# Moving the key one-hot turn, and the query turns behind it, one attention step on

## The chip, the cores and the metric

The kernel runs on one core of a Trainium2 chip. The time is that of the device for one execution, in microseconds (us); the median over several executions is quoted. "PE" is the matmul engine, "DVE" the vector engine, "ACT" the scalar engine, "POOL" gpsimd and "SP" the sync engine, which here only issues transfers.

## The reference

Clustered attention (4 batches, 8 heads, 768 positions, head size 64, 16 clusters), then a mixture of 4 experts. The part that matters is how a query sees only the keys of its own cluster:

```python
q_assign = np.argmax(np.einsum('bhsd,hcd->bhsc', q_n, c_n), axis=-1)
k_assign = np.argmax(np.einsum('bhsd,hcd->bhsc', k_n, c_n), axis=-1)
mask = q_assign[:, :, :, None] == k_assign[:, :, None, :]
scores = np.where(mask, scale * np.matmul(q, k.transpose(0, 1, 3, 2)), -1e9)
...
attn = np.exp(scores - max); attn = attn / (sum + 1e-9)      # then attn @ v
...
h = np.maximum(x @ w1[e], 0.0)                               # e = 0..3
out += p[:, e:e + 1] * (h @ w2[e])
```

## The kernel before

Every instruction stream is ordered by hand. The mask is folded into the score matmul: below the 64 rows of a key (tile `kf`) and a query (tile `qf`) lie 16 more rows with the one-hot of its cluster. To make them, the kernel scores positions against centroids, takes the maximum, compares (tile `oh`), transposes the one-hot on PE (the "turn") and copies the result from PSUM into rows 64 to 79. For the first batch this is side work, tied to attention steps.

```python
def onehot(self, shifts=1):                 # the key turn: 6 transposes for shifts=2
    self.ot = self.bank(BF16)
    for x in range(shifts):
        for c0 in range(0, self.w, 128):
            nc.tensor.matmul(self.ot[...], self.oh[:, c0 + x*CL : c0 + x*CL + 128], identb,
                             is_transpose=True)
def put(self, j, r, on): ...                # copy 16 rows of head j, half r, into kf (DVE or ACT)
def keep(self, on="dve"):                   # copy the whole turned tile into SBUF tile oht
    self.oht = asg.tile([128, QW], BF16, name="oht", bufs=2)
    self.move(self.oht[:, :self.w], self.ot[:, :self.w], on)
def send(self, j, r):                       # a transfer from oht into the rows of kf
    (... nc.sync).dma_start(out=self.rows(slice(D, D + CL), j, r), in_=self.oht[...])
# ... onehot_narrow, put_narrow: the same for one query block, 8 transposes and DVE copies
```

`k1` is the keys of heads 4 to 7 (local heads 0 to 3), `qb` the first query block of these heads, `qc` more queries of heads 0 to 3. So heads 4 and 5 get their rows by DVE copies (`puts`, two each), heads 6 and 7 by four transfers from `oht`.

One attention step is two (later four) score matmuls into one of two score banks `ps_s`, an exp on ACT into tile `at`, and the four value matmuls of the step two earlier (`LAG = 2`):

```python
for x, (h, y) in enumerate(...): nc.tensor.matmul(sp[...], KF..., QF...)   # score bank, 2 buffers
nc.scalar.activation(at, sp, ACT.Exp, scale=scale)
queue.append(pv); flush(LAG); tick()
# ...
at_step = {
    # ...
    5: lambda: (k1.back(), k1.top(), qb.back(), qb.top(), ...),
    7: lambda: (k1.onehot(2), puts(k1, 0), k1.keep(), k1.send_all((2, 3))),
    8: lambda: (qb.onehot_narrow(), qb.put_narrow(slice(0, 2), "dve")),
    9: lambda: (puts(k1, 1), qb.put_narrow(slice(2, HG), "dve")),
    11: lambda: qc.turn(0, dve, True),
    12: lambda: (qc.turn(1, dve, True), load_w(1)),
    14: lambda: (casts(qc, (0, 1)), qc.scores(dve)),
    # ...
}
while step < 3 * PER_U // 4 + LAG + D_T:
    at_step.pop(step, lambda: None)()       # side work of this step first,
    one_step()                              # then the next attention step
```

The softmax here doesn't subtract the row's maximum and nothing guards it: scores larger than these inputs give would overflow.

Of the kernel before, what the change touches and what calls it, by code (L numbers as in the profile page):

```python
# [20 lines left out]
def kernel(  # L21
# [27 lines left out]
    HG = H // 2  # L49
# [24 lines left out]
    act, dve, pool = nc.scalar.copy, nc.vector.tensor_copy, nc.gpsimd.tensor_copy  # L74
# [732 lines left out]
    k0, k1 = Assign(0, 1, 0, ("s", "mo", "mo", "mo")), Assign(0, 1, 1, ("s", "misc"))  # L807
    qa, qb = Assign(0, 0, 0, ("av",), 0, 1), Assign(0, 0, 1, ("mo",), 0, 1)
# [26 lines left out]
    def puts(x, j):  # L835
        for r in range(2):
            x.put(j, r, "dve")
# [27 lines left out]
    def late_casts():  # L865
        for j in range(HG):
            cast_v(0, 1, (j,))
            if j < 2:
                casts(k1, (2 + j,))
# [4 lines left out]
        3: lambda: (k1.scores(act), qb.scores(dve), puts(k0, 3)),  # L874
        5: lambda: (k1.back(), k1.top(), qb.back(), qb.top(),
                    qb.cast(0, 0, pool), qb.cast(0, 1, pool), late_casts()),
        7: lambda: (k1.onehot(2), puts(k1, 0), k1.keep(), k1.send_all((2, 3))),
        8: lambda: (qb.onehot_narrow(), qb.put_narrow(slice(0, 2), "dve")),
        9: lambda: (puts(k1, 1), qb.put_narrow(slice(2, HG), "dve")),
        11: lambda: qc.turn(0, dve, True),  # L880
        12: lambda: (qc.turn(1, dve, True), load_w(1)),
        14: lambda: (casts(qc, (0, 1)), qc.scores(dve)),
# [81 lines left out]
```

## Time and profile before

| | before |
|---|---|
| median of the first three runs | 472.22 us (472.22 to 472.25) |
| span of the profiled run | 470.4 us |
| PE busy | 463.2 us, 98% |
| holes of PE between 17 and 25 us | 0.41 (DVE's one-hot), 0.28 (ACT), 0.27 (a send) |

Besides the lines in the prediction, three of PE in the kernel before serve as marks below. In lines of the trace the columns are start in us, length in us, engine, line, operation, tiles, shape and count, and in brackets the idle time before the line and what ended it.

```profile
14.95 0.43 PE L267 MATMUL ps_mo<-t32q,bdc 128*32 128x128 f32 x8
...
22.91 0.78 PE L267 MATMUL ps_mo<-t32q,bdc 128*32 128x256 f32 x8
...
26.72 0.23 PE L692 MATMUL ps_mo<-identb,xn 128*128 128x128 bf16 x1 [0.28 <-DVE xn L685]
```

The first is the narrow query score matmul, the last shared landmark before the moved work (from here on "the mark"); the last is an output transpose (it turns a finished attention tile `xn`) after all of it. I call the time from the one to the other **the stretch**: 26.72 - 14.95 = 11.77 us here. It leaves out most of how a run started. The middle line is the next query score matmul, which reads two query copies of DVE (`t32q`).

### The profile page before, as it was taken

Reading aid. Unit: us, or ns where it says so; the run is one execution under the profiler, and the core shown is the slowest. Engines: PE = TensorE matmul, PEld = TensorE weight load, DVE = VectorE, ACT = ScalarE, POOL = GpSimd, SP = SyncE. Lnnn points to the kernel's source line nnn. Section 1 sums busy time; section 2 is a strip of 40 time slices with the busy share of each in tenths; the row PEclk is TensorE's granted clock in tenths of the full one; section 3 lists DMA queues with packets and bytes.
Section 4 is the critical chain, followed back from the end, with each engine's and each line's share of the span. In section 5 each row is a group of like instructions: output and inputs, shape, how many; then the busy total and the mean of one; then the engine's idle time right before and its main releaser. Section 6 shows DMA issues by size and latency. Waiting matters only on the chain.

```text
span 470.4 us, 11349 instructions
## 1 busy us (share of the span) xinstructions
PE 463.2 (98%) x4505; PEld 329.1 (70%) x4505; DVE 227.4 (48%) x554; ACT 276.9 (59%) x502; POOL 194.8 (41%) x301
## 2 busy tenths in 40 slices
PE   8999999999999999999999999999999999999996
PEld 5778777767767766777776667766766666667665
DVE  5964723542325563321234463523778767674112
ACT  5767675445655655566565656656665675664342
POOL 5936779275355593450433942000233232230000
PEclk9999999999999999999999999999999999999999
DMA  8999966996645941503666844220100100100101
GB/s 277 262 211 339 216 99 120 236 127 182 144 68 127 182 114 32 144 18 61 169 123 127 133 106 151 71 75 11 52 13 8 54 11 10 33 29 11 46 2 45
DMA packets 82381, 49.85 MB, mean 106 GB/s; under 512 B 57944, under 2 KB 77080, under 8 KB 82328
## 3 DMA queue, kind: packets, MB, share of 16 engines
q1 hardware_dynamic: 73080, 39.80, 35.1%
q0 software_dynamic: 8576, 9.25, 11.0%
q8 instruction: 35, 0.57, 0.5%
q14 instruction: 18, 0.15, 0.1%
q10 hardware_dynamic: 672, 0.08, 0.1%
HBM read 37.31 MB, written 6.30 MB: 93 GB/s over the span
## 4 chain that ended last, share of the span: by engine, by line
PE 95%; DVE 2%; DMA 1%; issue 0%; ACT 0%; SPq 0%; ACTq 0%
PE ps_mo L739 36%; PE ps_mo L758 35%; PE ps_s L649 9%; PE ps_av L676 7%; PE ps_s L562 1%; DMA kf<-oht 1%; PE ps_misc L562 1%; PE ps_s L87 1%; PE ps_mo L406 1%; PE ps_mo L242 1%; PE ps_misc L406 1%; DVE kf L315 1%; PE ps_misc L242 1%; PE ps_mo L267 0%; PE ps_misc L267 0%; DVE oh L287 0%
## 5 line engine op out<-in xcount | busy, mean ns | idle before, releaser
L655 ACT ACTIVATE at<-ps_s 128x512 bf16<-128x512 f32 x252 | 147.6, 596 | 115.5 <-PE ps_s L649 100.1
L739 PE MATMUL ps_mo<-xT,w1b 128*128 128x256 bf16 (+1 forms) x1664 | 195.9, 264 | 0.0
L758 PE MATMUL ps_mo<-w2b,hT 128*128 128x512 bf16 (+2 forms) x784 | 190.0, 375 | 0.0
L739 PEld LDWEIGHTS <-w1b 128*128 128x128 bf16 x1664 | 146.1, 98 | 24.8 <-issue 1.2
L745 ACT ACTIVATE hT<-ps_mo 128x512 bf16<-128x512 f32 x192 | 114.7, 598 | 60.5 <-PE ps_mo L739 57.7
L767 DVE SCALAR_TENSOR_TENSOR oacc<-ps_mo,psb,oacc 128x512 f32<-128x512 f32 (+1 forms) x74 | 54.3, 734 | 125.3 <-PE ps_mo L758 125.1
L758 PEld LDWEIGHTS <-hT 128*128 128x128 bf16 x784 | 66.9, 98 | 57.8 <-issue 3.1
L649 PE MATMUL ps_s<-qf,kf 80*128 80x256 bf16 (+1 forms) x456 | 82.7, 267 | 0.8 <-ACT at L655 0.4
L676 PEld LDWEIGHTS <-at 128*128 128x128 bf16 x1152 | 69.9, 97 | 15.3 <-issue 1.7
L676 PE MATMUL ps_av<-vx,at 128*128 128x65 bf16 x1152 | 80.3, 193 | 0.0
L662 POOL TENSOR_TENSOR at<-at,same 128x512 bf16<-128x512 bf16 x24 | 28.2, 1177 | 98.5 <-ACT at L655 83.0
L649 PEld LDWEIGHTS <-kf 80*128 80x128 bf16 x456 | 42.1, 98 | 20.6 <-issue 1.4
L380 POOL COPY t<-t 128x768 uint16<-128x768 uint16 x40 | 44.3, 1127 | 0.0
L579 DVE TENSOR_SCALAR same<-qf,late 128x256 bf16<-128x256 bf16 x144 | 39.0, 323 | 0.0
L662 DVE TENSOR_TENSOR at<-at,same 128x512 bf16<-128x512 bf16 x48 | 21.6, 450 | 25.9 <-ACT at L655 25.9
L364 POOL COPY h<-raw 128x768 uint16<-128x768 uint16 x24 | 20.3, 864 | 30.4 <-DMA raw<-in_k_dram 16.7
L361 POOL COPY h<-raw 128x768 uint16<-128x768 uint16 x16 | 13.1, 829 | 39.3 <-DMA raw<-in_q_dram 32.3
L765 DVE TENSOR_SCALAR oacc<-ps_mo,psb 128x512 f32<-128x512 f32 x18 | 13.5, 748 | 27.0 <-PE ps_mo L758 27.0
L683 DVE RECIPROCAL zr<-ps_av 128x4 f32<-128x4 f32 (+1 forms) x50 | 8.9, 178 | 33.3 <-PE ps_av L676 33.2
L336 POOL DMA_DIRECT2D qf<-oht x40 | 20.4, 519 | 7.5 <-DVE oht L313 3.9
L422 POOL COPY st<-sct 128x384 uint16<-128x384 uint16 x16 | 11.0, 736 | 28.8 <-DMA sct<-scs 28.8
L685 DVE TENSOR_TENSOR xn<-ps_av,zr 128x256 bf16<-128x256 f32 (+1 forms) x50 | 20.7, 414 | 1.7
(130 smaller groups left out, 263.2 us busy)
## 6 DMA issues: line engine op xcount, KB each, us to landing
raw<-in_v_dram SPq DMA_DIRECT2D x8, 768.0 KB, 5.4
out_dram<-oacc SPq DMA_DIRECT2D x23, 256.0 KB, 2.0
raw<-in_k_dram SPq DMA_DIRECT2D x7, 768.0 KB, 7.5
raw<-in_q_dram SPq DMA_DIRECT2D x6, 768.0 KB, 5.7
w1b<-in_moe_w_dram POOLq DMA_DIRECT2D x4, 1024.0 KB, 12.3
w2b<-in_moe_w_dram POOLq DMA_DIRECT2D x4, 1024.0 KB, 17.6
qf<-nos SPq DMA_DIRECT2D x2, 768.0 KB, 5.2
xT<-xn SPq DMA_TRANSPOSE x80, 2.4
```

The source lines that it names most:

```text
L336: (nc.gpsimd if self.b or self.i0 and self.g else nc.sync).dma_start(out=self.rows(slice(D, D + CL), j, r), in_=self.oht[p0:p0 + CL, :self.w])
L380: pool(self.all[:, y * w:(y + 1) * w].bitcast(U16)[:, z::2], self.t16[:, (2 * z + y) * w:(2 * z + y + 1) * w])
L579: nc.vector.tensor_scalar(same[:, x * 256:(x + 1) * 256], clusters(b)[:, g, w, k // 2, k % 2, :], key_nos[b % 2][:, g, 8 * i + 4 * (k // 2 ...
L649: nc.tensor.matmul(sp[:, x * n:(x + 1) * n], KF[b % 2][:K, h, r, i * 128:(i + 1) * 128], QF[b % 2][:K, h, rs[0]:rs[-1] + 1, w * 128:(w + 1 ...
L655: nc.scalar.activation(at, sp, ACT.Exp, scale=scale)
L662: (nc.gpsimd if n4 in POOL_STEPS else nc.vector).tensor_tensor(at, at, same_cluster(b, w, cur), op=ALU.mult)
L676: nc.tensor.matmul(av[:, h % 2, m, :], at[:, c0:c0 + 128], VX[b % 2][:, h, 2 * i + r, :], start=(first and x == 0 and m == 0), stop=(last ...
L685: nc.vector.tensor_tensor(xn[:, :nr].rearrange("p i j d -> p j i d"), av[:, :, :, :D], zr.broadcast_to([128, 2, nr, D]), op=ALU.mult)
L739: nc.tensor.matmul(ph[:, x * n:(x + 1) * n], W1[e][:, i, (f + x) * 128:(f + x + 1) * 128], xT[:, i, :], start=(i == 0), stop=(i == ND - 1))
L745: nc.scalar.activation(ht, ph, ACT.Relu)
L758: nc.tensor.matmul(po, hT[f // per][:, c0:c0 + 128], W2[e][:, f, c], start=(f == 0), stop=(f == NF - 1))
L767: nc.vector.scalar_tensor_tensor(oacc[:, c], po, pap, oacc[:, c], op0=ALU.mult, op1=ALU.add)
```

## The change

The intent is to fill the hole that PE has before the key turn: one step more of attention is issued ahead of it.

```diff
-        7: lambda: (k1.onehot(2), puts(k1, 0), k1.keep(), k1.send_all((2, 3))),
-        8: lambda: (qb.onehot_narrow(), qb.put_narrow(slice(0, 2), "dve")),
-        9: lambda: (puts(k1, 1), qb.put_narrow(slice(2, HG), "dve")),
+        8: lambda: (k1.onehot(2), puts(k1, 0), k1.keep(), k1.send_all((2, 3))),
+        9: lambda: (qb.onehot_narrow(), qb.put_narrow(slice(0, 2), "dve")),
+        10: lambda: (puts(k1, 1), qb.put_narrow(slice(2, HG), "dve")),
```

## The prediction

> **What bounds the kernel now.** I began with the page, to see which engine fills the span, and then cut the span into stretches to find where that engine is not full. The columns after the stretch are its length, then busy microseconds with the number of instructions for PE, PEld, DVE, ACT and POOL, then the granted clock, the DMA share and GB/s.
>
> ```profile
> PE 463.2 (98%) x4505; PEld 329.1 (70%) x4505; DVE 227.4 (48%) x554; ACT 276.9 (59%) x502; POOL 194.8 (41%) x301
> ...
> 16.00:20.00 4.00, 3.56 (x53) 3.04 (x51) 3.79 (x13) 2.90 (x6) 3.67 (x8) 1.00 1.11 233
> 20.00:24.00 4.00, 3.74 (x55) 3.09 (x55) 3.75 (x12) 2.97 (x6) 3.84 (x7) 1.00 1.20 213
> 24.00:24.75 0.75, 0.48 (x10) 0.29 (x7) 0.59 (x3) 0.60 (x1) 0.69 (x2) 1.00 1.26 214
> 24.75:28.00 3.25, 2.75 (x44) 2.23 (x45) 1.92 (x8) 2.52 (x5) 0.97 (x2) 1.00 1.20 214
> 28.00:60.00 32.00, 31.83 (x426) 25.83 (x426) 19.17 (x51) 21.21 (x40) 19.17 (x34) 1.00 1.11 254
> 60.00:120.00 60.00, 60.00 (x603) 43.73 (x602) 22.26 (x38) 34.04 (x60) 41.97 (x66) 1.00 0.79 149
> ```
>
> From 28 us on PE is filled almost without a hole, at full clock, so whatever PE gains or loses before that goes one for one into the end. The moved steps lie between 17 and 21 us. There PE has holes, while DVE (3.79 and 3.75 of 4.00) has nearly none and the DMA engines are full (share above 1). The third view is PE in order of time: start, length, instruction, and in brackets the idle time before it and what ended it.
>
> ```profile
> 16.88 0.38 PE L649 MATMUL ps_s<-qf,kf 80*128 80x256 bf16 x2
> 17.09 0.28 PE L676 MATMUL ps_av<-vx,at 128*128 128x65 bf16 x4
> 17.79 0.51 PE L296 MATMUL ps_misc<-identb,oh 128*128 128x128 bf16 x6 [0.41 <-DVE oh L287]
> 18.14 0.38 PE L649 MATMUL ps_s<-qf,kf 80*128 80x256 bf16 x2
> ...
> 20.26 0.38 PE L649 MATMUL ps_s<-qf,kf 80*128 80x256 bf16 x2 [0.28 <-ACT at L655]
> ...
> 24.75 0.22 PE L649 MATMUL ps_s<-qf,kf 80*128 80x128 bf16 x1 [0.27 <-DMA kf<-oht]
> ```
>
> The line at 17.79 is the moved turn: six transposes of the key one-hot (oh). PE stood 0.41 us before it because DVE had not finished oh. That hole is what the change aims at. Two more matter: 0.28 us for an exp of ACT at 20.26, and 0.27 us at 24.75 for rows of kf that come by DMA. The fourth view, the chain of waits through this stretch, tells which holes count.
>
> ```profile
> 17.18 0.57 DVE oh L287
> 17.75 0.05 issue
> 17.79 0.52 PE ps_misc L296 x6
> 18.31 0.02 issue
> 18.34 0.61 DVE kf L315 x2
> 18.95 0.01 issue
> 18.96 0.37 DVE oht L315
> 19.33 0.01 issue
> 19.35 0.62 SPq L336
> 19.97 0.04 issue
> 20.01 4.60 DMA kf<-oht
> 24.62 0.14 issue
> 24.75 0.22 PE ps_s L649
> ```
>
> The chain does not run along PE's attention work. It runs from oh through the moved turn, two copies into kf, the copy kept for the sends (oht), the sync engine's issue, and a transfer that takes 4.60 us to land, into the score matmul at 24.75.
>
> **What the Trainium skill says.** "Perfetto Trace Analysis", section "DMA Instruction — HWDGE (DVE, Sync)", says that the profiled length of such an issue leaves out the movement of data. The trace agrees: 0.62 us of issue, 4.60 us to landing. "DMA: Bandwidth & Descriptors", section "Issuing engines are not separate DMA queues", says that transfers from the scalar, sync and gpsimd engines interleave on the same 16 engines. That fits the full share while expert weights are loading by the software queue; it is my reading of why 12 KB needs 4.60 us. "TensorE: Matmul & The Clock Gate", its table of specifications, says that only weight loads are pulled ahead in TensorE's queue. The hole at 17.79, with the ready work of step 8 right behind it, is what this would give.
>
> **The change, part by part.** Three entries of the table that ties side work to attention steps move on by one: the key turn with its copies and four sends from 7 to 8, the first half of the narrow query turn from 8 to 9, the rest from 9 to 10. Nothing is added or removed. The compiled order says the same: PE has the same 8578 rows, ACT, POOL and SP are unchanged, and on DVE only one pair moves. An entry at n is issued just before step n+1, so one step (2 score matmuls, 4 value matmuls) moves ahead of the key turn, another ahead of the narrow turn, another ahead of the last entry. From the turn of the next queries at 20.60 on, PE's order is as before.
>
> *The hole at 17.79.* The step that moves forward takes PE about 0.35 us (0.40 from the scores at 16.48 to the next at 16.88, 0.35 from those at 15.31 to those at 15.66). But it can't start where the hole begins. There are two score banks, so step 8 writes the bank of step 6, whose exp must have ended. ACT in a short stretch shows:
>
> ```profile
> 16.23 1.26 ACT L655 ACTIVATE at<-ps_s 128x512 bf16<-128x512 f32 x2
> 16.90 1.08 ACT L655 ACTIVATE at<-ps_s 128x512 bf16<-128x512 f32 x2
> ```
>
> The second of the first pair is the first of the second pair: step 6's exp, from 16.90 to 16.23 + 1.26 = 17.49. With 0.05 us for the release (step 7's scores start at 16.88, an exp after 16.23 + 0.60 = 16.83), step 8's scores start at 17.54. The scores' issue takes 17.09 - 16.88 = 0.21 us, and the four value matmuls 0.12 us (from 15.54 and 19.35 to what follows them; once, at 18.36, it is 0.21). So the key turn can start at 17.54 + 0.33 = 17.87. oh lets it start at 17.79. The hole is filled, and the turn is 0.08 us later.
>
> *The hole at 20.26.* ACT now has step 8's scores about 0.4 us sooner, so I expect this 0.28 us to vanish too. PE then reaches 20.60's work about 0.35 + 0.28 = 0.6 us early.
>
> *DVE.* Before the key copies it is free at 18.25 (17.96 + 0.29) and starts them at 18.34. It would start at 18.42, and oht, the issues and the transfers all slip by 0.08 us. A reciprocal and a product (0.18 + 0.42 us) then pass ahead of the copies for head 5, which end near 21.1 and not 20.41; head 5 is read at about 22.5, so nothing waits. DVE has the same sum to do and reaches the query copies of 21.42 and 22.32 as late as before.
>
> *The transfer.* Four sends go out at 0.6 us pitch and land 0.6 us apart: by the same 4.6 us the second, third and fourth would land near 24.6, 25.2 and 25.9, which is where the score matmuls of heads 6 and 7 stop in the trace. All work up to 24.75 is the same in both kernels. So the 0.6 us that PE has won is spent waiting there: the hole of 0.27 becomes about 0.8 us, and the matmul starts near 24.83.
>
> *Sum.* -0.35 -0.28 (holes closed), +0.63 (waiting for the same transfer), +0.08 (the transfer later): +0.08 us, 472.22 to 472.3.
>
> **Rivals.** (a) The transfers don't bind: the PE gain stays, and the time falls by up to 0.41 + 0.28 = 0.69 us to 471.5. For it: these are real PE holes and PE bounds the rest. Against it: PE already waits for kf at 24.75, so arriving sooner cannot help. (b) The turn goes a whole step later, with oht and the sends: +0.35 to +0.5 us, to 472.7. For it: the change reads so. Against it: the step fits into the hole but for 0.08 us. It would take an exp that is late. (c) The transfers meet the weight load differently. They queue behind bulk loads, so 0.1 us in the issue may become some tenths in the landing, either way: 472.0 to 472.7. (d) A bank or DVE becomes the wait: the narrow turn and the last copies come later, and the second query turn needs the bank that head 5's copies read until about 21.1. PE could then stand there, but all before 24.75 is covered by the transfer.
>
> **Range and chances.** The runs before lie within 0.03 us, so the range is about mechanism: 471.9 (part of rival a, or a luckier landing) to 472.7 (b or c). I predict 472.3 us. Two per cent is 9.4 us; all holes of this stretch together are far below it. Faster by over 2%: 0.01; within 2%: 0.98; slower: 0.01.
>
> **What would show it.** Right: the key turn without a hole over 0.1 us before it and starting at 17.8 to 17.9; no ACT wait near 20; DVE's oht ending near 19.4; a wait of 0.6 to 1.0 us for kf before a score matmul at 24.7 to 24.9; after it the same picture as before, shifted by under 0.2 us. Wrong: no larger wait for kf, or kf landing by more than 0.3 us elsewhere, or a new hole after 28 us, which I expect nowhere.

## The result, and the profile after

The changed kernel took 472.66 us (median of 4 runs: 472.24, 472.51, 472.82, 472.92), the kernel before 472.24 us (4 runs, 472.22 to 472.28). The ratio is 1.0008, with a 95% interval of 0.9991 to 1.0025: the same at 2%, and not told apart from no change at all. (A ratio is the mean time of one kernel's fast runs over that of the other's of the same rounds, so not quite the ratio of the medians.) All outputs are right. The profiled run was the slowest of the four, 472.92 us, with a span of 471.1 us. PE in it:

```profile
15.25 0.43 PE L267 MATMUL ps_mo<-t32q,bdc 128*32 128x128 f32 x8
...
17.84 0.38 PE L649 MATMUL ps_s<-qf,kf 80*128 80x256 bf16 x2 [0.17 <-ACT at L655]
...
18.18 0.50 PE L296 MATMUL ps_misc<-identb,oh 128*128 128x128 bf16 x6
...
21.52 0.66 PE L242 MATMUL ps_misc<-ident,raw 128*128 128x128 f32 x4 [0.24 <-DVE kf L315]
...
22.80 1.38 PE L267 MATMUL ps_mo<-t32q,bdc 128*32 128x256 f32 x8
...
25.12 0.22 PE L649 MATMUL ps_s<-qf,kf 80*128 80x128 bf16 x1 [0.21 <-DMA kf<-oht]
...
26.75 0.33 PE L649 MATMUL ps_s<-qf,kf 80*128 80x128 bf16 x3 [0.45 <-DMA kf<-oht]
...
27.09 0.23 PE L692 MATMUL ps_mo<-identb,xn 128*128 128x128 bf16 x1
```

The key turn has no hole before it any more; the score matmul ahead of it waited 0.17 us for an exp of ACT. The ACT wait of 0.28 us that came near 20 us is gone. So PE did win time. It lost it again in three places that were not there before or were smaller: 0.24 us before the second query turn, whose bank head 5's copies still read; about 0.6 us inside the query score matmuls (1.38 us and not 0.78); and two waits for sends.

The longer query score matmuls are explained by DVE. Its two query copies, first in the kernel before, then in the changed one:

```profile
21.42 0.68 DVE L252 COPY t32q<-ps_mo 128x512 f32<-128x512 f32 x1
22.32 0.69 DVE L252 COPY t32q<-ps_misc 128x512 f32<-128x512 f32 x1
```

```profile
21.95 0.69 DVE L252 COPY t32q<-ps_mo 128x512 f32<-128x512 f32 x1
22.81 0.68 DVE L252 COPY t32q<-ps_misc 128x512 f32<-128x512 f32 x1
```

Counted from each run's own mark, they start at 6.47 and 7.37 us before, at 6.70 and 7.56 us after: DVE is 0.2 us later, while PE came 0.4 us earlier (22.91 - 14.95 = 7.96 against 22.80 - 15.25 = 7.55). PE started these matmuls early and stood in the middle of them until the second copy was done at 23.49.

Of the 0.70 us between the two profiled spans (471.1 - 470.4), 0.30 lie before the change has begun (15.25 - 14.95). The stretch is 27.09 - 15.25 = 11.84 us, 0.07 longer. Then 0.20 come between that output transpose and the next (26.72 to 28.35 before, 27.09 to 28.92 after), behind the last send, which landed late. The remaining 0.13 us are spread over the rest and I have no cause for them.

The 0.30 us are in the very first matmuls, which are the same in both kernels. Nine fp32 transposes of keys, before and after:

```profile
4.63 1.74 PE L242 MATMUL ps_mo<-ident,raw 128*128 128x128 f32 x9
```

```profile
4.58 2.08 PE L242 MATMUL ps_mo<-ident,raw 128*128 128x128 f32 x9
```

In both, single matmuls of this shape take about 0.42 us at first and 0.27 us from some moment on; the moment is later in the second trace. The Trainium skill, "TensorE: Matmul & The Clock Gate", section "What's actually happening", says that the clock is released by a free-running activity window, so that the release varies from run to run. The durations fit this, but the granted-clock column reads 1.00 here, so I call it the likely cause and not a shown one.

### The profile page after: what moved, and what is told of

It reads as the page before. It is cut to its first block, busy times and chain, and to the rows that moved or that the text cites. A ratio compares the mean times of both kernels' runs of the same rounds, so it can differ in the third digit from the quotient of the medians.

```text
span 471.1 us, 11349 instructions
## 1 busy us (share of the span) xinstructions
PE 463.6 (98%) x4505; PEld 329.6 (70%) x4505; DVE 227.7 (48%) x554; ACT 277.0 (59%) x502; POOL 194.7 (41%) x301
## 4 chain that ended last, share of the span: by engine, by line
PE 96%; DVE 1%; DMA 1%; SPq 0%; issue 0%; ACT 0%
PE ps_mo L739 36%; PE ps_mo L758 35%; PE ps_s L649 10%; PE ps_av L676 8%; PE ps_s L562 1%; DMA kf<-oht 1%; PE ps_mo L242 1%; PE ps_misc L562 1%; PE ps_s L87 1%; PE ps_mo L406 1%; PE ps_misc L267 1%; PE ps_misc L242 1%; PE ps_mo L267 1%; PE ps_misc L406 1%; PE ps_mo L276 0%; SPq L336 0%
```

## The experiments

The differences are 0.1 us in 472, and a run's start moves by more, so the stretch is the main reading and the median the second. What the start or the stretch gains does come through one for one, as the prediction assumed: in 12 of the 14 traces the span ends 443.7 us (within 0.1) after the stretch does. The two others are the first trace of the changed kernel (444.0, the late last send) and the run with later sends (445.0, see there). Some of the short stretches below belong to late marks, so pairs with like marks weigh most. "Largest landing" is the longest time from issue to landing among the four sends of `kf`. All were timed in 5 rounds (6 runs for one of them); the kernel before ran 38 times in all, 472.04 to 473.04, median 472.22.

| run | mark at | key turn after mark | stretch | largest landing | median |
|---|---|---|---|---|---|
| before | 14.95 | 2.84 | 11.77 | 4.7 | 472.24 |
| before again (e10) | 14.86 | 2.84 | 11.89 | 4.7 | 472.22 |
| changed | 15.25 | 2.93 | 11.84 | 5.0 | 472.66 |
| changed again (e1) | 15.22 | 2.93 | 11.93 | 5.1 | 472.45 |
| changed again (e9) | 14.72 | 2.93 | 11.96 | 4.9 | 472.30 |
| key turn alone (e2) | 14.83 | 2.93 | 11.92 | 4.8 | 472.27 |
| queries alone (e3) | 14.96 | 2.84 | 11.69 | 4.6 | 472.25 |
| changed, sends first (e4) | 15.24 | 2.93 | 11.47 | 4.7 | 472.21 |
| before, sends first (e5) | 14.83 | 2.83 | 11.79 | 5.7 | 472.09 |
| before, sends first (e11) | 15.40 | 2.84 | 11.29 | 4.7 | 472.21 |
| key turn alone, sends first (e6) | 15.06 | 2.93 | 11.36 | 4.7 | 471.94 |
| key turn alone, sends first (e12) | 15.11 | 2.93 | 11.36 | 4.8 | 471.96 |
| before, sends later (e7) | 14.89 | 2.84 | 12.49 | 5.0 | 473.28 |
| changed, sends first, head 5 on ACT (e8) | 15.32 | 2.93 | 11.25 | 4.7 | 472.03 |

The theory under test: the sends (one-hot, key turn, copies, `oht`, four issues, landing) end last in this stretch, and the change delays them by the 0.08 us by which the key turn slips. The main rival: DVE's order and the bank (reciprocal and product ahead of head 5's copies, later query copies) set the end.

### The changed kernel again, and the kernel before again

No edit.

> The changed kernel unaltered, for the scatter of its time and a second trace. Theory (the sends of heads 6 and 7 set the time up to 26 us; the change delays them by 0.08 us): median 472.2 to 472.4 us, and the fast runs that lie above it do so because PE's clock comes up 0.3 us later, before the change begins. Rival (the change itself costs 0.4 us through a late fourth landing or DVE): median 472.5 to 472.8, and in the trace everything up to 15 us as in the kernel before, with the loss between 18 and 29 us.

> The changed kernel a third time, for its scatter. Its stretch from the narrow query score matmul near 15 us to the output transpose near 26.7 us was 11.84 and 11.93 us. If the change costs 0.1 to 0.2 us there, this trace shows 11.8 to 12.0; the median lies at 472.3 to 472.6, and what the trace has above 472.35 is a later start (over 15.0 us at that matmul) or a send that lands late.

> The kernel before once more as a control for a single trace: the stretch 11.7 to 11.85 us, the start anywhere from 14.8 to 15.3. If its stretch is as long as the changed kernel's (11.9 or more), the difference of 0.1 us that I read between them is scatter.

The changed kernel gave 472.45 us (472.29 to 472.98) and 472.30 us (472.15 to 472.71), the kernel before 472.22 us (472.11 to 473.04). The first of these lies between the two expectations for it, 472.2 to 472.4 and 472.5 to 472.8, and decides neither. Over all runs the changed kernel has a median of 472.385 us (14 runs) and the kernel before 472.22 (38). The three stretches of the changed kernel average (11.84 + 11.93 + 11.96) / 3 = 11.91, the two of the kernel before 11.83: 0.08 us. But one trace of the kernel before, 11.89, lies among those of the changed one, so by the expectation for that control most of a single trace's difference is scatter. Only the key turn's slip is free of it: 2.84 us in every trace with it at step 7 (2.83 once), 2.93 in every trace with it at step 8.

The start is scatter too. The late one of the second trace of the changed kernel has another cause than the first: there PE waited for keys to arrive.

```profile
6.08 0.55 PE L242 MATMUL ps_mo<-ident,raw 128*128 128x128 f32 x3 [0.58 <-DMA raw<-in_k_dram]
```

In the third trace the mark is at 14.72, the earliest of all, so the change does not cause late starts. That trace also lacks the late last send, and its waits are the plainest picture of the changed kernel:

```profile
17.65 0.50 PE L296 MATMUL ps_misc<-identb,oh 128*128 128x128 bf16 x6
...
20.99 0.66 PE L242 MATMUL ps_misc<-ident,raw 128*128 128x128 f32 x4 [0.24 <-DVE kf L315]
...
22.27 1.37 PE L267 MATMUL ps_mo<-t32q,bdc 128*32 128x256 f32 x8
...
24.71 0.22 PE L649 MATMUL ps_s<-qf,kf 80*128 80x128 bf16 x1 [0.18 <-DMA kf<-oht]
```

The send's wait is 0.18 us, less than in the kernel before, since DVE has already held PE back by 0.24 + (1.37 - 0.78) = 0.83 us.

### The key turn alone

```diff
-        7: lambda: (k1.onehot(2), puts(k1, 0), k1.keep(), k1.send_all((2, 3))),
-        8: lambda: (qb.onehot_narrow(), qb.put_narrow(slice(0, 2), "dve")),
+        8: lambda: (k1.onehot(2), puts(k1, 0), k1.keep(), k1.send_all((2, 3)),
+                    qb.onehot_narrow(), qb.put_narrow(slice(0, 2), "dve")),
```

> Only the key turn with its copies and sends goes one step on; the narrow query turn and the last copies keep their steps 8 and 9, so DVE's order is that of before. Theory of the sends: the hole before the key turn closes, the sends leave 0.05 to 0.1 us later, the hole before the kf rows grows instead; 472.3 us, as the whole change. Rival (DVE's new order, reciprocal and product ahead of head 5's copies, costs the time): 472.2 here, with no PE wait on DVE for the second query turn.

472.27 us (472.15 to 472.67), a stretch of 11.92. The hole before the key turn closes as in the changed kernel, the turn is 0.09 us later, and with DVE's order untouched the stretch is as long as the changed kernel's. So the longer stretch, as far as it is longer than the 11.89 of the kernel before at all, does not need DVE's new order. The hole before the kf rows grew no larger, however: 0.26 us, with 0.28 for ACT near 20 us still there and a new wait of 0.33 us for DVE at an output transpose.

### The queries alone

```diff
-        8: lambda: (qb.onehot_narrow(), qb.put_narrow(slice(0, 2), "dve")),
-        9: lambda: (puts(k1, 1), qb.put_narrow(slice(2, HG), "dve")),
+        9: lambda: (qb.onehot_narrow(), qb.put_narrow(slice(0, 2), "dve")),
+        10: lambda: (puts(k1, 1), qb.put_narrow(slice(2, HG), "dve")),
```

> Only the query entries and the last copies go one step on; the key turn stays at step 7. Theory of the sends: they leave as in the kernel before, so 472.2 us within 0.1, although PE waits for DVE at the second query turn. Rival (DVE's order and the bank are the cost): 472.4 to 472.7 us.

472.25 us (472.11 to 472.35), a stretch of 11.69. The rival asked for 472.4 to 472.7 and falls as the sole cause: DVE's later query copies alone cost nothing. They show, though: the query score matmuls take 1.37 us as in the changed kernel, and the profile shows no wait for a send before the score matmuls of head 6, because PE reaches them late (the rows also landed a little sooner than usual, 4.5 to 4.6 us after issue). Their group takes 0.48 us where 0.39 is usual, so about 0.1 us of waiting is hidden in it. Two chains of nearly equal length end here.

### Sends first

DVE copies `oht` ahead of head 4's rows, so the four sends leave 0.6 us sooner.

```diff
-        8: lambda: (k1.onehot(2), puts(k1, 0), k1.keep(), k1.send_all((2, 3))),
+        8: lambda: (k1.onehot(2), k1.keep(), k1.send_all((2, 3)), puts(k1, 0)),
```

> The changed kernel with the copy for the sends and the sends ahead of head 4's two copies on DVE; PE's order is untouched. Theory of the sends: they leave 0.6 us sooner, the waits for kf at 24.7 to 26.7 us shrink or go, and the PE time won by the change now counts: 471.7 us (0.3 to 0.6 below the changed kernel). Rival (DVE's query copies bound this stretch): within 0.1 us of the changed kernel, with the holes moved to the wait for the query copies.

472.21 us (471.96 to 472.54), 0.24 below the changed kernel of the same rounds (472.45), and not the 471.7 I wanted. The start of the traced run was late (15.24); the stretch is 11.47, 0.44 below the changed kernel's mean and 0.37 below its trace with the same start (15.25, 11.84). So the sends do set the end of the changed kernel. The miss tells where the rest is. The chain of waits of this run, up to the first line start, length, what:

```profile
20.83 0.62 DVE kf L315 x2
...
21.48 0.42 DVE qf L313
...
21.94 0.69 DVE t32q L252
...
22.63 0.26 DVE xT L697 x2
22.89 0.61 DVE t32q L252
...
23.54 0.62 PE ps_mo L267 x4
```

It now runs over DVE's copies with no gap over 0.04 us: the rival's chain is the next in line.

The same edit in the kernel before (step 7), twice, and with the key turn alone moved (step 8, queries untouched), twice:

> The kernel before with the copy for the sends and the sends ahead of head 4's copies; PE's order as in the kernel before. Since the start of a run scatters by 0.3 us or more, the reading is the stretch from the narrow query score matmul near 15 us to the output transpose near 26.7 us: 11.77 us in the kernel before, 11.84 and 11.93 in the two traces of the changed one, 11.47 with the sends first in the changed one. Theory of the sends: they leave 0.6 us sooner, the wait for kf goes, and the stretch is 11.3 to 11.45 us; median about 471.8 us. Rival (in the kernel before the query copies of DVE are as late as the sends): 11.6 us or more.

> The sends first with the key turn at step 7, a second time. The first trace missed: 11.79 us and not 11.3 to 11.45, since the first send took 5.73 us to land where the others took 4.6 to 4.7. If that landing was scatter, this trace has a landing below 5 us and a stretch of 11.3 to 11.5; if a send that is issued earlier merely lands as late as before, it has again a landing over 5.3 and a stretch of 11.7 to 11.8.

> Only the key turn one step on, with the sends first: closed hole, early sends, DVE's order otherwise of before. If PE's own work bounds the stretch once the sends are early, it is 0.1 to 0.3 us shorter than the same with the key turn at step 7, 11.1 to 11.2 us. If DVE bounds it, the later key turn (0.09 us) is all that shows: 11.4 to 11.5 us.

> Only the key turn one step on, the sends first, a second time: the stretch 11.36 us again within 0.1 if DVE and PE bound it once the sends are early; median 471.8 to 472.1.

The first of these missed: 472.09 us (471.94 to 472.17), but a stretch of 11.79. PE waited for the first send, which left early and took 5.7 us to land. The second fence gives the four sends of this trace (the expectation for the repeat, written from a count that held other sends too, calls only the first one late; the median shows that it was not alone):

```profile
24.46 0.40 PE L649 MATMUL ps_s<-qf,kf 80*128 80x128 bf16 x4 [0.32 <-DMA kf<-oht]
```

```profile
DMA to landing us min/median/max: 4.7/5.3/5.7
```

The repeat has a largest landing of 4.7, no wait for a send, and a stretch of 11.29 (472.21 us, 472.10 to 472.42, with the latest start of all, 15.40). With that start its sends left at 19.17 us of the run, where those of the first left at 18.60, so the pair does not tell scatter from an effect of the moment of issue. The two traces told of next settle part of it: their sends left at 18.91 and 18.96 us and landed within 4.8 us of issue. So an early send can land early, and landings scatter between 4.5 and 5.7 us after issue over these traces, enough to hide or fake an effect of this size.

With the key turn at step 8 and the sends first, both traces have 11.36 and the medians are 471.94 and 471.96 us (together 471.74 to 472.44, ten runs). That met the expectation of DVE as the next bound (11.4 to 11.5) nearly, and that of PE (11.1 to 11.2) not: of PE's lines one waits for DVE where the kernel before had no hole.

```profile
21.75 0.28 PE L692 MATMUL ps_mo<-identb,xn 128*128 128x128 bf16 x2 [0.33 <-DVE xn L685]
```

Against 11.29 with the turn at step 7 the stretch shows no gain by the move of the key turn, even where no send is waited for. That comparison is weak: the trace with 11.29 started latest of all, the other trace with the turn at step 7 has 11.79, and by the medians of ten runs each the version with the turn moved is 0.18 us faster (471.95 against 472.13 us). Whether the move gains something once the sends are early stays open. By the median this version is 0.27 us below the kernel before and 0.4 below the changed one, the best that I ran; its ratios to the kernel before (0.9994 and 0.9992, intervals 0.9982 to 1.0006 and 0.9979 to 1.0004) do not prove a gain.

### Head 5 on ACT

On top of the changed kernel with sends first:

```diff
-        10: lambda: (puts(k1, 1), qb.put_narrow(slice(2, HG), "dve")),
+        10: lambda: (k1.put(1, 0, "act"), k1.put(1, 1, "act"), qb.put_narrow(slice(2, HG), "dve")),
```

> The changed kernel with the sends first and head 5's two copies on ACT and not on DVE. If DVE's query copies bound the changed kernel once the sends are early, they come 0.6 us sooner, the long stall of the query score matmuls (1.38 us, 0.78 before) goes, and the stretch is 11.0 to 11.2 us, median 471.6. If ACT's exps are pushed back by the two copies (0.85 us) instead, PE waits for ACT and the stretch stays at 11.4 to 11.6 us.

472.03 us (471.88 to 472.18), a stretch of 11.25, between the two expectations. The query score matmuls take 0.64 us, so their stall was indeed DVE's copies. PE pays part of it elsewhere, for ACT:

```profile
21.59 0.66 PE L242 MATMUL ps_misc<-ident,raw 128*128 128x128 f32 x4 [0.23 <-ACT kf L311]
```

### Sends later

In the kernel before, head 5's copies go ahead of `oht`: the same DVE instructions, permuted.

```diff
-        7: lambda: (k1.onehot(2), puts(k1, 0), k1.keep(), k1.send_all((2, 3))),
+        7: lambda: (k1.onehot(2), puts(k1, 0), puts(k1, 1), k1.keep(), k1.send_all((2, 3))),
-        9: lambda: (puts(k1, 1), qb.put_narrow(slice(2, HG), "dve")),
+        9: lambda: qb.put_narrow(slice(2, HG), "dve"),
```

> The kernel before with head 5's two copies ahead of the copy for the sends: the same instructions on DVE in another order, the sends 0.63 us later, the query copies where they were. Theory of the sends: the delay goes through, the stretch becomes 12.2 to 12.5 us and the median 472.7 to 472.9. Rival (the sends don't set the end of this stretch): 11.7 to 11.9 us and 472.2.

The stretch is 12.49 us, 0.66 above the mean of the kernel before, for sends that leave 0.63 us later: the delay goes through whole, and the sends do set the end in the kernel before. The median missed upwards: 473.28 us, with runs from 472.66 to 476.04. In the traced run (474.15 us) PE's holes were followed by a drop of its clock. The columns are the stretch, its length, busy us and instructions of PE, PEld, DVE, ACT and POOL, then granted clock, DMA share and GB/s.

```profile
24.00:26.00 2.00, 1.02 (x14) 0.73 (x12) 0.43 (x3) 0.84 (x2) 1.57 (x3) 1.00 1.25 212
...
28.00:31.00 3.00, 3.00 (x35) 2.83 (x33) 1.87 (x8) 2.32 (x5) 0.00 (x0) 0.50 1.12 210
...
31.50:32.00 0.50, 0.50 (x10) 0.49 (x8) 0.27 (x2) 0.37 (x1) 0.00 (x0) 1.00 1.14 197
```

PE ran at half clock from about 28 to 31 us, just as its work resumed. Three us at half clock can cost up to 1.5 us, and this run is 474.15 - 472.22 - 0.66 = 1.27 us above the kernel before with the delay, so the drop suffices for the rest. Only this run is traced, but the record has the mean granted clock of every run. It is 0.996 for this one and 0.993 for the one of 476.04 us, which fits such a drop there too. The runs of 473.07 and 473.49 us have 0.999, no lower than many runs of the kernel before, so for them a drop is not shown.

## Why the prediction was right or wrong

**The time and the range.** 472.66 us lies within 471.9 to 472.7, though near its end, and "within 2%" was right, as it would have been under any of the rivals, since all the holes in question are under 1 us. The point of 472.3 is nearer to what later rounds gave (472.45, 472.30, and 472.385 over all). I took the scatter from runs that lay within 0.03 us; over 38 runs it is 1.0 us. What the first result has above 472.3 is, in its trace, mostly a late start (0.30) and a late landing of the last send (0.20).

**The hole at 17.79.** Right. The score matmul waited for the exp, and the key turn slipped by 0.09 us where 0.08 was worked out. One reading on the way is loose: the prediction calls step 8 "ready work" behind the hole, but by its own sums step 8 is ready only from 17.54. What the page says of weight loads in the queue no run here tests. The prediction's count of 8578 rows is from the compiled program.

**The hole at 20.26.** Right: the ACT wait went. The experiment with the key turn alone keeps it and the one with the queries alone loses it, so it is the moved query turn that does this.

**DVE.** Half right. `oht` ended 0.07 us later from the mark (19.33 - 14.95 = 4.38, 19.70 - 15.25 = 4.45). But "DVE has the same sum to do and reaches the query copies of 21.42 and 22.32 as late as before" failed: they came 0.23 and 0.19 us later. 0.07 of it is the later `oht`; another 0.11 is that the product `xn` overlapped by 0.07 with the query copy behind it (21.07 + 0.42 = 21.49 against 21.42), while now head 5's copies follow it after a gap of 0.04 (20.38 + 0.42 = 20.80 against 20.84). The remaining 0.05 I have no cause for.

**The transfer.** The step "the hole of 0.27 becomes about 0.8 us" failed: 0.21, 0.27 and 0.18 us in the three traces. "No larger wait for kf" was one of the prediction's own signs of being wrong, and it came. The waits hidden inside the next score groups did not grow either: groups of four that take 0.39 us unhindered took 0.49 and 0.60 before, 0.41 and 0.63 in the third trace. The won time was taken back a little sooner, by DVE: 0.24 us for the bank and 0.6 us inside the query score matmuls. This is the wait that rival (d) named, with the reservation that the send covers it. The reservation held for the end: with DVE's order of before (the key turn alone) the stretch is as long. That the send sets the end was right: sends 0.63 us later made the stretch 0.66 longer, sends earlier made it 0.44 shorter in the changed kernel. The reading that the full DMA engines hold the sends up fits the trace of the kernel before: there sends of the same 12 KB, issued by gpsimd, landed after 1.6 to 1.7 us from 200 to 203 us, at a DMA share of 0.18, and after 3.6 to 4.7 us from 100 to 104 us, at 1.13. No experiment varied the load.

**The sum.** +0.08 us against a mean difference of the stretches of 0.08. The agreement is better than the data: single traces of one kernel differ by 0.12. What is firm is that the PE holes closed by the change (0.41 to 0.17, 0.28 to none) did not shorten the stretch.

**The rivals.** (a), a gain of up to 0.69 us, is out. (b), a whole step's delay of the turn, is out: 0.09 us. (c), a landing that shifts by tenths, is part of the scatter and of the first result. (d) is where PE waits now, but it does not by itself lengthen anything, as the queries alone show.

## What to carry to other kernels

Before filling a hole of the busiest engine, follow the chain past the hole to the next thing that engine must wait for: time won ahead of a transfer that has not been sent sooner is only waited for later, on whichever of two nearly equal chains comes first. Here what moved the stretch was the order of three copies on DVE, the one that feeds the transfers first, and not the place of the matmuls alone; no gain in the time of the whole kernel is proven for either. For effects of 0.1 us in 470, compare a stretch between two landmarks in several traces, since start and landings scatter by more than the effect.

## What the Trainium skill lacked or had wrong

- "TensorE: Matmul & The Clock Gate" (section "What's actually happening") ties the throttled state to an idle window of about 3.4 us. In the traced run with later sends PE was not idle so long at a time: it was busy 1.02 of 2.00 us from 24 to 26 us with single holes of at most 0.72 us, and the granted clock still fell to 0.50 from 28 to 31 us. Another section of the page ("A second HAM failure mode: psum-queue depth-cycling") does tell of short idles that bring the throttle back, but not how much idle time is enough. Here PE was busy 1.61 of the 3 us from 24 to 27 us; in the first trace of the changed kernel it was busy 2.34 of them and the clock stayed at 1.00. That the holes caused the drop is likely and, from one trace, not shown.
- "DMA: Bandwidth & Descriptors" gives about 2.0 us of fixed cost for one DMA of the gpsimd path (section "Anatomy of one DMA — SWDGE (gpsimd) path"). The sends of 12 KB by gpsimd at 200 to 203 us, with the DMA engines at a share of 0.18, landed even sooner, after 1.6 to 1.7 us. These 12 KB sends within SBUF, issued from the sync engine while weights load on the other queue, took 4.5 to 5.7 us to land, with 1.0 us between the quickest and the slowest of the four in one trace. No page that I read says how far small transfers are held up and scattered by a bulk load.
